# Attention and feed-forward on one core: last tokens in blocks of 256 and 128, zeros written first, one order table replaced by another

## The chip, the cores and the metric

The kernel runs on one core of a Trainium2 chip. A core has five engines with an instruction queue each: PE (the matrix engine, which writes only to PSUM), DVE and ACT (elementwise work), POOL (elementwise work and one kind of DMA) and SP (which here only issues DMAs). They meet through semaphores. Sixteen DMA engines move data between the main memory (HBM) and the on-chip memory (SBUF). The metric is the device time of one execution in microseconds (us), median over the runs of one kernel.

## The reference

Four batches of 1088 tokens, four heads of 32 values each. The attention is linear: a feature map of 64 features per token and head is formed from two projections to 8 values, and so there is no softmax. The result of the attention, 4352 tokens of 128 values, goes through two matrix products with a squared ReLU between them.

```python
def _attn_ref(q, k, v, S1, S2):
    def phi(x):
        a = np.einsum('rd,bhsd->bhsr', S1, x)
        b = np.einsum('rd,bhsd->bhsr', S2, x)
        return np.einsum('bhsi,bhsj->bhsij', a, b).reshape(*x.shape[:-1], r * r)
    q_p, k_p = (phi(q), phi(k))
    kv = np.einsum('bhsf,bhsd->bhfd', k_p, v)
    z = np.sum(k_p, axis=2)
    num = np.einsum('bhsf,bhfd->bhsd', q_p, kv)
    den = np.einsum('bhsf,bhf->bhs', q_p, z)[..., None] + 1e-06
    return num / den

def _moe_ref(x, w_in, w_out):          # x: 4352 x 128, w_in: 128 x 2048, w_out: 2048 x 128
    r = np.maximum(x @ w_in, 0.0)
    return (r * r) @ w_out
```

## The kernel before

**Attention, per batch b (0 to 3).** The steps have names which the order table uses, with the batch as their first number. `ldk`, `ldq`, `ldv` load k, q and v (SP queue, lines 334, 349, 359). `tk` and `tq` transpose k and q on DVE (L380, L442). `ksk` multiplies k by the projections on PE (L390), `kk` transposes the result back (L396) and `kp` forms the 64 features of k on DVE, two instructions of 128x1152 for a batch (L402). `vp` copies v into the layout that the next product needs, a column of ones beside it: two halves for a batch, of three instructions each (L368 and twice L370). `kv` is the product of features and v on PE (L418), `kve` copies it out (L434). For batches 0 and 1 the features of q come from PE: `qr` (L456), a copy `qa` on ACT (L468), a product `qp` on DVE (L473), in three groups of tokens. For batches 2 and 3 they come through the memory: `qr`, `ab` on ACT, `wr` writes a scratch tensor, `rda` and `rdb` read it back spread out (tiles qp and Bq, L512 and L518), `qp` multiplies (L526). `num` is the product with kv (L576), `mx` divides (three DVE instructions, L599 to L601), `tx` transposes on PE (L614) and `xe` copies to xT, the input of the feed-forward, in bf16 (L619).

**Feed-forward, by blocks of tokens.** `SIZES` gives the blocks n = 0, 1, ...: 384, seven of 512, 384. For each block the 16 slices of 128 hidden values are taken W at a time, W = 2 for blocks of more than 256 tokens and W = 4 for smaller ones: `m1.n.m` is W matmuls with w_in into one PSUM tile h of 1024 columns (L642; three such tiles, h0 to h2), `r.n.m` the ReLU from h into an SBUF tile r (ACT, L654, or DVE, L656), `g.n.m` the square (DVE, L669, or ACT, L667), `m2.n.m` W matmuls with w_out that add into the one PSUM tile o (L675). When all are in, `oe` transposes o into an SBUF tile osb on DVE (L682) and four stores `st` (one for each group of 32 partitions, L692) write the block out, more where a block crosses a batch.

**What sets the order.** Nothing is scheduled at run time. The table `PLAN` names every step once, in the order in which it is emitted, with its engine and the buffers it takes; each engine runs its own instructions in that order and waits where a semaphore has not come. A DMA takes one of eight semaphores in turn (DMAHW0 to DMAHW7), whichever of the queues of SP and ACT issues it, and waits until the DMA before it on that semaphore has landed. The last instruction waits for all of them.

**The start.** PE first runs products of a tile of zeros (`heat`, L274), 15 of them around the first work, which need only `zero` (DVE, L212). `ident` (DVE, L228) needs `iota` from POOL. POOL sets constants (`kz`, `z`, `mk`), waits for the first loads with `gate` (L282), issues the loads of the weights w_in (`win`, L285) and w_out (`wout`, L289) on its own DMA queue, and lets the loads of batch 1 and later go with small writes into their targets (`mark0` for k of batch 1, `mark1` for the others, L296).

## Time and profile before

| | before |
|---|---|
| runs: median, lowest, highest | 112.34, 112.20, 112.92 us |
| the profiled execution: its time | 112.42 us |
| its span, first to last instruction | 110.4 us |
| DMA queue of SP and ACT (q1, q10) | 13.95 MB |
| DMA queue of POOL (q0) | 1.05 MB |
| read from and written to HBM | 13.25 MB, 2.79 MB |

The profiled execution lies 0.08 us above the median of the runs, and its span lies 2.0 us below its own time; these 2.0 us are before the first and behind the last instruction. In a row of the timeline stand the start (us from the span's start), the time that the row's instructions took, the engine, the line, the operation, what it writes and reads, and their count; in square brackets how long the engine had been idle before it, and what ended that. "SPq" and "ACTq" are the queues' own work of issuing DMAs. A row of grouped instructions has the busy time, the mean of one in ns, and behind the bar the idle time before them.

### The profile page before, as it was taken

The numbers are of one execution on the slowest core, as the hardware profiler recorded it, in microseconds if no ns is written. First come the engines' busy times: TensorE is split into PE (matmuls) and PEld (weight loads), VectorE is DVE, ScalarE is ACT, GpSimd is POOL, SyncE is SP. The second block draws the span as 40 slices with busy tenths as digits, with TensorE's granted clock in tenths as the row PEclk, the third lists the DMA queues.
The fourth block names the chain that finished last, engine by engine and source line by source line (L and its number), as shares of the span: only waits on it lengthen the run. The fifth ranks groups of instructions, "written<-read, shape, count | busy, mean of one in ns | idle before, by whom it ended". The sixth has DMA issues, their size and how long they took to land.

```text
span 110.4 us, 3529 instructions
## 1 busy us (share of the span) xinstructions
PE 95.6 (87%) x1424; PEld 54.4 (49%) x1436; DVE 94.4 (85%) x157; ACT 86.3 (78%) x111; POOL 19.3 (18%) x59
## 2 busy tenths in 40 slices
PE   0993766999989899999999999998999999999900
PEld 0332754664546557475449354465665444445400
DVE  1439976899999999999999999999899899998720
ACT  5006044899899798899999899999999999999500
POOL 5019990001910280000007200000000000000000
PEclk9999999999999999999999999999999999999995
DMA  2698989994288867576764269720045112041542
GB/s 85 187 232 171 208 181 195 308 270 128 69 212 290 260 195 223 207 215 154 195 159 173 63 167 221 130 39 6 0 85 86 22 29 49 3 71 21 86 82 36
DMA packets 27456, 15.22 MB, mean 138 GB/s; under 512 B 19888, under 2 KB 23344, under 8 KB 27440
## 3 DMA queue, kind: packets, MB, share of 16 engines
q1 hardware_dynamic: 25248, 13.80, 48.2%
q0 software_dynamic: 992, 1.05, 7.0%
q10 hardware_dynamic: 1200, 0.15, 0.8%
q8 instruction: 11, 0.18, 0.7%
q14 instruction: 5, 0.04, 0.1%
HBM read 13.25 MB, written 2.79 MB: 145 GB/s over the span
## 4 chain that ended last, share of the span: by engine, by line
PE 45%; DMA 16%; DVE 13%; POOL 7%; ACT 5%; issue 5%; SPq 3%; POOLq 0%; ACTq 0%
PE o L675 21%; PE h L642 16%; DMA qin<-in_q_dram 6%; ACT r L654 5%; DMA kin<-in_k_dram 4%; DMA qp<-scr 4%; DMA vin<-in_v_dram 3%; PE h L576 3%; DVE kp L402 2%; POOL vp L370 2%; DVE qp L526 2%; DVE g L669 2%; DVE qp L473 2%; DVE osb L682 2%; POOL w_out L289 2%
## 5 line engine op out<-in xcount | busy, mean ns | idle before, releaser
L654 ACT ACTIVATE r<-h 128x1024 bf16<-128x1024 f32 (+1 forms) x64 | 59.2, 976 | 2.5 <-PE h L642 1.6
L642 PE MATMUL h<-xT,w_in 128*128 128x512 bf16 (+1 forms) x136 | 36.3, 367 | 1.7 <-ACT xT L619 0.6
L675 PE MATMUL o<-g,w_out 128*128 128x512 bf16 (+1 forms) x141 | 35.0, 367 | 0.6 <-issue 0.3
L669 DVE TENSOR_TENSOR g<-r 128x1024 bf16<-128x1024 bf16 (+1 forms) x54 | 33.2, 650 | 1.3 <-PE o L675 0.9
L642 PEld LDWEIGHTS <-w_in 128*128 128x128 bf16 x144 | 15.6, 114 | 15.4 <-issue 3.5
L675 PEld LDWEIGHTS <-w_out 128*128 128x128 bf16 x144 | 13.6, 98 | 15.2 <-issue 2.2
L667 ACT ACTIVATE g<-r 128x1024 bf16<-128x1024 bf16 (+1 forms) x18 | 18.3, 1023 | 0.1
L402 DVE TENSOR_TENSOR kp<-kk 128x1152 f32<-128x1152 f32 x8 | 11.7, 1485 | 0.1
L368 POOL COPY vp<-vin 128x512 f32<-128x512 f32 x7 | 5.1, 723 | 35.7 <-DMA Bq<-scr 17.4
L656 DVE TENSOR_SCALAR r<-h 128x1024 bf16<-128x1024 f32 (+1 forms) x8 | 9.5, 1187 | 0.5 <-PE h L642 0.4
L418 PE MATMUL a<-vp,kp 128*32 128x33 f32 (+1 forms) x504 | 7.1, 201 | 1.9 <-DVE kp L402 1.7
L418 PEld LDWEIGHTS a<-vp,kp 128*32 128x32 f32 (+1 forms) x504 | 6.5, 113 | 3.4 <-ACT A L468 2.0
L370 POOL COPY vp<-vtl 32x64 f32<-32x64 f32 x14 | 7.7, 551 | 0.4
L274 PE MATMUL o<-zero 128*128 128x512 bf16 x15 | 5.2, 507 | 2.5 <-DVE zero L212 2.5
L468 ACT COPY A<-h 128x384 f32<-128x384 f32 (+1 forms) x12 | 5.1, 463 | 2.8 <-issue 1.6
L682 DVE STREAM_TRANSPOSE osb<-o 128x512 f32<-128x512 f32 (+1 forms) x9 | 6.1, 681 | 1.3 <-PE o L675 1.3
L456 PE MATMUL h<-qT,SR 32*64 32x192 f32 (+1 forms) x192 | 5.8, 325 | 1.2 <-DVE qT L442 0.9
L473 DVE TENSOR_TENSOR qp<-h,A 128x384 f32<-128x384 f32 (+1 forms) x12 | 6.1, 526 | 0.9 <-ACT A L468 0.9
L380 DVE STREAM_TRANSPOSE kT<-kin 128x1024 f32<-128x1024 f32 (+1 forms) x5 | 5.1, 1017 | 1.9 <-DMA kin<-in_k_dram 1.9
L576 PE MATMUL h<-kvz,qp 128*64 128x66 f32 (+1 forms) x144 | 6.1, 224 | 0.0
L576 PEld LDWEIGHTS h<-kvz,qp 128*64 128x64 f32 (+1 forms) x144 | 5.2, 135 | 1.0 <-issue 0.4
L442 DVE STREAM_TRANSPOSE qT<-qin 128x1088 f32<-128x1088 f32 (+2 forms) x5 | 5.3, 1061 | 0.0
(64 smaller groups left out, 74.2 us busy)
## 6 DMA issues: line engine op xcount, KB each, us to landing
qp<-scr SPq DMA_DIRECT2D x8, 272.0 KB
Bq<-scr SPq DMA_DIRECT2D x16, 136.0 KB
vin<-in_v_dram SPq DMA_DIRECT2D x16, 128.0 KB
qin<-in_q_dram SPq DMA_DIRECT2D x6, 272.0 KB
kin<-in_k_dram SPq DMA_DIRECT2D x4, 288.0 KB
kin<-in_k_dram SPq DMA_DIRECT2D x4, 256.0 KB
out_dram<-osb SPq DMA_DIRECT2D x16, 64.0 KB
scr<-ab SPq DMA_DIRECT2D x8, 68.0 KB
```

The costliest lines, as they stand in the source:

```text
L370: fn(vp[i][32 * c : 32 * c + 32, h, NJ - 1, 0:D], vtl[b][:, h, c])
L402: en.tensor_tensor(out=kp[i][:, pr].rearrange("p j h (x y) -> p (j h) x y", x=R), in0=t[:, :, 1][:, :, None, :].to_broadcast([128, 2 * NJ, ...
L418: nc.tensor.matmul(at(vb)[p : p + m, 33 * pr : 33 * pr + 33], kp[i][:, pr, j, h, m * f : m * f + m], vp[i][:, 2 * pr + h, j, :], start=(j ...
L473: nc.vector.tensor_tensor(out=qp[i][:, pr, t0 : t0 + 2 * n].rearrange("p (m s) -> p m s", m=2), in0=at(hb[pr]).rearrange("p (m s) -> p m s ...
L576: nc.tensor.matmul(t[32 * cc : 32 * cc + 32 * w, 2 * pr : 2 * pr + 2, :], qp[i][:, pr, 32 * c : 32 * c + 32 * w], (kvs if sw else kvz)[b][ ...
L642: nc.tensor.matmul(at(hb)[:, col(w) : col(w) + N], w_in[:, 512 * (ct // E) : 512 * (ct // E) + 512].rearrange("p (c e) -> p e c", e=E)[:, ...
L654: nc.scalar.activation(o, i_, ACTF.Relu)
L656: nc.vector.tensor_scalar_max(o, i_, 0.0)
L667: nc.scalar.activation(at(gb)[:, 0:tot], r, ACTF.Square)
L669: nc.vector.tensor_tensor(out=at(gb)[:, 0:tot], in0=r, in1=r, op=ALU.mult)
L675: nc.tensor.matmul(at(ob)[:, 0:N], w_out[:, ct, :], at(gb)[:, W * N * (mm % SQ_W) + N * w : W * N * (mm % SQ_W) + N * w + N], start=(ct == ...
L682: nc.vector.transpose(at(sbuf)[:, 0:N], at(ob)[:, 0:N])
```

## The change

Five things. `SIZES`: the last block of 384 tokens becomes one of 256 and one of 128; both take W = 4, so that a ReLU or a square of the block of 256 is 1024 columns wide and of the block of 128 is 512. `VP_ENG`: both halves of `vp` of batch 0 stand on ACT, where the second was on POOL. `ident` is kept behind `zero` on DVE. The stores of the last block alternate between the queues of SP and ACT. And `PLAN` is another table: other steps change their engines too (`SKq` goes from DVE to POOL, `xe0.0` from ACT to DVE, the four `kve` of batch 0 swap engines, more of the `xe` stand on ACT), and most steps stand in another place.

```diff
-VP_ENG = "POOL|ACT"
+VP_ENG = "ACT"
-SIZES = [384, 512, 512, 512, 512, 512, 512, 512, 384]
+SIZES = [384, 512, 512, 512, 512, 512, 512, 512, 256, 128]
 PLAN = """
-ldk0.16:SP kz0:POOL z0:POOL iota:POOL ident:DVE zero:DVE heat0:PE:o0 heat1:PE tk0.16:DVE mk:POOL warm:ACT heat2:PE heat3:PE heat4:PE heat5:PE heat6:PE
+zero:DVE heat0:PE:o0 heat1:PE heat2:PE heat3:PE heat4:PE heat5:PE heat6:PE heat7:PE heat8:PE heat9:PE ldk0.16:SP warm:ACT lds0:SP lds1:SP heat10:PE
...
-        ident, iot, 0, op=ALU.is_equal), [o_iota], n=128)
+        ident, iot, 0, op=ALU.is_equal), [o_iota], n=128, after=[o_zero])
...
-                add(f"st{n}.{lo}.{db}", "SP|ACT" if n == len(SIZES) - 1 else "SP", f_st, [o_oe], uses=[sbuf], n=128 * (hi_ - lo))
+                add(f"st{n}.{lo}.{db}", ("SP", "ACT")[db % 2] if n == len(SIZES) - 1 else "SP", f_st, [o_oe], uses=[sbuf], n=128 * (hi_ - lo))
```

Three places of the new order follow, each before and after. The rows give the line, the operation, what it writes and reads (with buffer numbers) and the shape; "x2" is two alike in a row.

First place, the start, on POOL from `gate` on. Before:

```order
L282 COPY gate_147<-vin0_115 64x1
L285 DMA w_in_104<-in_moe_w_in_dram 128x512
L285 DMA w_in_104<-in_moe_w_in_dram 128x1024
L285 DMA w_in_104<-in_moe_w_in_dram 128x512
L296 MEMSET kin1_108 128x2
L368 COPY vp0_127<-vin0_115 128x2x8x32
L370 COPY vp0_127<-vtl0_119 32x2x32 x2
L252 MEMSET vp1_128 128x36
L253 MEMSET vp1_128 64x4x33
L254 MEMSET kT1_124 128x2x32
L289 DMA w_out_105<-in_moe_w_out_dram 128x512
```

And after:

```order
L282 COPY gate_147<-vin0_115 64x1
L285 DMA w_in_104<-in_moe_w_in_dram 128x512 x2
L285 DMA w_in_104<-in_moe_w_in_dram 128x1024
L296 MEMSET kin1_108 128x2
L289 DMA w_out_105<-in_moe_w_out_dram 128x512
L289 DMA w_out_105<-in_moe_w_out_dram 128x2x512
L289 DMA w_out_105<-in_moe_w_out_dram 128x512
L296 MEMSET vin1_116 128x1
L296 MEMSET vtl1_120 32x1
L296 MEMSET qin1_112 128x2
L296 MEMSET kin2_109 128x2
```

The copies of v have left POOL, the three memsets of `z1` stand ahead of `gate` now, and the loads of w_out and the writes of `mark1` follow the loads of w_in at once.

The same place on DVE, which opens with `zero`, as the difference of the two orders:

```order
 L746 UNCONDITIONAL_BRANCH
+L212 MEMSET zero_102 128x256
 L228 TENSOR_SCALAR ident_95<-iot_94 128x128
-L212 MEMSET zero_102 128x256
 L380 STREAM_TRANSPOSE kT0_123<-kin0_107 128x2x256
 L382 STREAM_TRANSPOSE kT0_123<-kin0_107 128x2x32
```

`zero` no longer stands behind `ident`, which needs POOL's `iota`.

Second place, the SP queue around the scratch reads of batch 2 (tiles Bq0 and qp0 from scr0). Before:

```order
L498 DMA scr0_145<-ab0_143 32x2x272
L334 DMA kin2_109<-in_k_dram 128x512
L512 DMA qp0_139<-scr0_145 128x1x544
L518 DMA Bq0_141<-scr0_145 64x1x544
L512 DMA qp0_139<-scr0_145 128x1x544
L518 DMA Bq0_141<-scr0_145 64x1x544
L512 DMA qp0_139<-scr0_145 128x1x544
L334 DMA kin3_110<-in_k_dram 128x512
L518 DMA Bq0_141<-scr0_145 64x1x544 x5
L498 DMA scr1_146<-ab1_144 32x2x272
```

And after:

```order
L518 DMA Bq0_141<-scr0_145 64x1x544 x2
L359 DMA vtl3_122<-in_v_dram 32x4x64
L692 DMA out_0_dram<-osb0_78 32x12x32
L518 DMA Bq0_141<-scr0_145 64x1x544 x2
L512 DMA qp0_139<-scr0_145 128x1x544
L518 DMA Bq0_141<-scr0_145 64x1x544 x2
L692 DMA out_0_dram<-osb0_78 32x12x32
L512 DMA qp0_139<-scr0_145 128x1x544
L518 DMA Bq0_141<-scr0_145 64x1x544 x2
L512 DMA qp0_139<-scr0_145 128x1x544
```

A store of block 0, which waits for `oe0`, stands after the second of the twelve reads now; before, the first store stands behind all twelve.

Third place, the end of the SP queue, with the semaphores that each waits for. Before:

```order
L692 DMA out_0_dram<-osb3_81 32x16x32 [waits DMAHW2_49]
L692 DMA out_0_dram<-osb2_80 32x10x32 [waits DMAHW3_49]
L692 DMA out_0_dram<-osb2_80 32x6x32 [waits DMAHW4_49]
L692 DMA out_0_dram<-osb1_79 32x12x32 [waits DMAHW5_49,DVE_49]
L746 UNCONDITIONAL_BRANCH
```

And after:

```order
L692 DMA out_0_dram<-osb0_78 32x8x32 [waits DMAHW4_49,DVE_49]
L692 DMA out_0_dram<-osb0_78 32x8x32 [waits DMAHW5_49]
L692 DMA out_0_dram<-osb0_78 32x8x32 [waits DMAHW6_49]
L692 DMA out_0_dram<-osb0_78 32x8x32 [waits DMAHW7_49]
L692 DMA out_0_dram<-osb3_81 32x4x32 [waits DMAHW0_49,DVE_49]
L692 DMA out_0_dram<-osb3_81 32x4x32 [waits DMAHW1_49]
L746 UNCONDITIONAL_BRANCH
```

The same place on ACT. Before:

```order
L654 ACTIVATE r3_74<-h1_64 128x768 [waits DVE_49,PE_49]
L654 ACTIVATE r0_68<-h2_65 128x768 [waits DVE_49,PE_49]
L692 DMA out_0_dram<-osb1_79 32x12x32 [waits DMAHW4_49,DVE_49]
L692 DMA out_0_dram<-osb1_79 32x12x32 [waits DMAHW6_49]
L692 DMA out_0_dram<-osb1_79 32x12x32 [waits DMAHW0_49]
L746 UNCONDITIONAL_BRANCH
```

And after:

```order
L654 ACTIVATE r4_76<-h1_64 128x512 [waits DVE_49,PE_49]
L667 ACTIVATE g3_75<-r2_72 128x512 [waits Activation_49]
L654 ACTIVATE r0_68<-h2_65 128x512 [waits DVE_49,PE_49]
L692 DMA out_0_dram<-osb3_81 32x4x32 [waits DMAHW7_49,DVE_49]
L692 DMA out_0_dram<-osb3_81 32x4x32 [waits DMAHW0_49]
L746 UNCONDITIONAL_BRANCH
```

Before, ACT's first store holds DMAHW4, and the next to last SP store waits for it. After, ACT's two stores hold DMAHW7 and DMAHW0, and two of the last three SP stores wait for them, the first of these a store of the block of 256.

## The prediction

> **What bounds the kernel now.** I read the busy times by stretches first, then the timeline of the start and of the end, the chain of waits, and last the groups of instructions for prices. The stretches (us of the span; their length, busy times and counts of PE, PEld, DVE, ACT, POOL; granted clock, DMA share, GB/s):

> ```profile
> 10.00:20.00 10.00, 6.49 (x175) 5.07 (x169) 8.17 (x15) 3.81 (x12) 6.12 (x20) 1.00 0.99 188
> 20.00:40.00 20.00, 18.46 (x405) 11.20 (x409) 19.43 (x34) 18.47 (x28) 5.29 (x10) 1.00 0.74 216
> 80.00:100.00 20.00, 19.86 (x123) 10.36 (x122) 18.97 (x29) 19.61 (x23) 0.00 (x0) 1.00 0.30 50
> 100.00:110.40 10.40, 4.91 (x29) 2.64 (x26) 4.63 (x9) 3.62 (x6) 0.00 (x0) 0.89 0.32 54
> ```

> From 20 on three engines are full together: DVE first (19.43 of 20), PE later (19.86 of 20). The waste lies at the ends: before 20, where PE and ACT stand idle, and behind 105. In between an order can save little, and an engine that gets more work costs about that much. So the sum has three parts: when the feed-forward starts, what is added behind it, and the end.

> **The start.** The timeline's rows up to the first feed-forward product:

> ```profile
> 2.18 0.27 DVE L212 MEMSET zero<- 128x256 uint32 x1
> 2.51 4.79 PE L274 MATMUL o<-zero 128*128 128x512 bf16 x14 [2.51 <-DVE zero L212]
> 5.60 0.71 DVE L380 STREAM_TRANSPOSE kT<-kin 128x512 f32<-128x512 f32 x1 [0.82 <-DMA kin<-in_k_dram]
> 7.22 0.43 PE L390 MATMUL a<-kT,SKk 64*32 64x288 f32 x1
> 8.05 0.48 DVE L396 STREAM_TRANSPOSE kk<-h 128x288 f32<-128x288 f32 x1 [1.74 <-PE h L390]
> 8.46 0.54 DVE L442 STREAM_TRANSPOSE qT<-qin 128x384 f32<-128x384 f32 x1
> 9.25 0.62 ACT L368 COPY vp<-vin 128x512 f32<-128x512 f32 x1 [4.49 <-DMA vin<-in_v_dram]
> 9.39 3.52 DVE L402 TENSOR_TENSOR kp<-kk 128x1152 f32<-128x1152 f32 x2
> 9.78 0.51 ACT L370 COPY vp<-vtl 32x64 f32<-32x64 f32 x2
> 10.28 2.73 POOL L370 COPY vp<-vtl 32x64 f32<-32x64 f32 x2
> 10.31 0.86 ACT L468 COPY A<-h 128x384 f32<-128x384 f32 x2
> 13.40 0.90 DVE L442 STREAM_TRANSPOSE qT<-qin 128x704 f32<-128x704 f32 x1
> 17.00 0.17 DVE L599 TENSOR_SCALAR den<-a 128x12 f32<-128x12 f32 x1
> 17.47 0.56 DVE L601 TENSOR_TENSOR xs<-a,rec 128x384 bf16<-128x384 f32 x1
> 18.90 0.89 DVE L473 TENSOR_TENSOR qp<-h,A 128x320 f32<-128x320 f32 x2 [0.87 <-ACT A L468]
> 19.30 1.14 PE L642 MATMUL h<-xT,w_in 128*128 128x384 bf16 x6 [0.62 <-ACT xT L619]
> ```

> The reader sees PE still busy with products of zeros at 7.30 (2.51 + 4.79), while the transposed k that `ksk0` needs is there at 6.31. And the eight `kp` (shortest, median and longest in ns):

> ```profile
> L402 DVE TENSOR_TENSOR kp<-kk x8: 1318/1356/2215, 9.4 to 70.3; 128x1152 f32<-128x1152 f32 x8
> ```

> *Zeros first.* `zero` no longer waits for `iota`; DVE can write it at about 0.75, where the first engines start, and the products of zeros then end at about 1.05 + 4.8 + one more of up to 0.43 = 6.3, when k is there: 0.87 earlier than now (7.22 against 6.35). The bound below is nothing, if PE runs its zeros slower; above, it cannot pass the arrival of k. I take 0.87. `kk` then starts at about 7.1 and `kp0` at 8.55.

> *The second half of `vp0` on ACT.* This costs ACT 0.62 + 0.51 = 1.13, so its first `qa` moves from 10.31 to about 11.4. DVE meets that only behind `kp0`. On POOL two copies of 32x64 took 2.73 while DVE ran `kp`, and the first `kp` took 2.2 against a median of 1.36; without the copies I price the two `kp` at 2.7 in place of 3.52. Bounds: a gain of 0.8, or nothing, if the issue of weight loads beside them slows DVE as well. I take the gain: the slow rows lie beside copies. [...]

> *The walk.* `kp0` ends at 8.55 + 2.7 = 11.25, not 12.91. `qa` is done at 11.85, so DVE waits 0.6, then does a `qp` (0.89/2 for 320 columns, some 0.55 for 384), the large `tq` (0.90), a second `qp` and two `kve` (0.22 each, a row further down): 14.3. `num0.0` and one `qp` with its copy bring it to 15.3, `mx` (17.00 to 18.03 now, 1.0) to 16.3, `tx` and `xe` to 17.1. The feed-forward starts at about 17.1 in place of 19.30: 2.2 earlier. DVE reaches the same point with `xe0.0` done as well (0.32, which was ACT's) and two `qp` left, as now: 1.85 earlier, from 18.90 to 17.05. The loads of w_out move ahead by nearly 4 us and run beside those of w_in; the DMA issues behind them cost POOL nothing that anybody waits for, and w_in has this time:

> ```profile
> w_in<-in_moe_w_in_dram POOLq DMA_DIRECT2D x2, 128.0 KB, 4.9
> w_in<-in_moe_w_in_dram POOLq DMA_DIRECT2D x1, 256.0 KB, 5.5
> ```

> Issued by 9.7, all of w_in lands by about 15.2, 1.9 before it is needed. That cover is what the earlier w_out could use up.

> **What is added behind the start.** Prices (by shapes, and in the chain of waits: start, time, what):

> ```profile
> L669 DVE TENSOR_TENSOR g<-r 128x1024 bf16<-128x1024 bf16 x41 | 26.6, 683 | 1.2 <-PE o L675 0.9
> L656 DVE TENSOR_SCALAR r<-h 128x1024 bf16<-128x1024 f32 x7 | 8.5, 1220 | 0.1
> L656 DVE TENSOR_SCALAR r<-h 128x768 bf16<-128x768 f32 x1 | 1.0, 957 | 0.4 <-PE h L642 0.4
> L619 DVE COPY xT<-a 128x704 bf16<-128x704 bf16 x1 | 0.5, 519 | 0.0
> ```

> ```profile
> 85.40 0.41 PE a L614 x6
> 96.15 0.86 PE o L675 x4
> 100.02 0.33 PE h L642 x2
> ```

> DVE: its squares grow by 2304 columns, at 26.6/41 = 0.65 for 1024 some 1.5 (1.7 with the smaller shapes' fixed part); one more ReLU of 512 columns, extrapolated from 1.22 and 0.96 to 0.7; from batch 0's second `xe` on two copies of 704 columns fewer, -1.0; two `kve` fewer, -0.45; one more `oe`, 0.2. Sum +1.1. ACT gets less, by the same columns, some 1.3, and is not the bound. PE: a matmul of 384 columns takes 0.165, one of 512 0.215. For 256 I interpolate 0.115; for 128 the transposes, which load new weights each time as well, give 0.41/6 = 0.068. The block of 384 cost 32 x 0.165 = 5.3; now 32 x (0.115 + 0.068) = 5.9: +0.6. Bounds: +0.3 by the slope alone (0.05 for 128), and +1.8 if each of the last 32 waits for its weights at about 0.1. I take 0.6, from the row with the same shape. [...]

> **The end.** The last rows of the timeline, and, of the SP queue's own waits (us in total, times, longest), that of a store for a store:

> ```profile
> 101.24 0.72 DVE L682 STREAM_TRANSPOSE osb<-o 128x512 f32<-128x512 f32 x1 [0.32 <-PE o L675]
> ...
> 104.95 0.58 DVE L682 STREAM_TRANSPOSE osb<-o 128x384 f32<-128x384 f32 x1 [0.57 <-PE o L675]
> 105.56 1.43 ACTq L692 DMA_DIRECT2D out_dram<-osb  x3
> 107.30 0.80 SPq L692 DMA_DIRECT2D out_dram<-osb  x2
> ```

> ```profile
> SPq L692 <- DMA out_dram<-osb: 2.3, 1, 2.3
> ```

> SP stands idle until 107.30, because a store ahead of the last one needs the semaphore of ACT's first store, which lands 1.74 after its issue. The end comes 2.3 after SP's last issue (108.10), 4.9 after the last `oe`. The new table keeps this: ACT's two stores hold DMAHW7 and DMAHW0, and SP has three stores behind them. Issues are shorter (four columns of 32 in place of twelve, 0.3 each against 0.4 to 0.5), so SP issues at 1.5, 1.9 and 2.3 after the last `oe` and the end comes at about 4.75: a gain of 0.15, with -0.3 and +0.5 as bounds. Ahead of it the last steps are smaller: by the two `oe` rows (0.72 for 512, 0.58 for 384) the last falls to some 0.3. But `m2.9` must wait for `oe8` (0.45) to empty the one tile o and then for squares of 0.4 each on DVE, and PE idles some 0.5 there which it did not before. I count these two as +0.2.

> **The sum.** From 105.53, the last `oe`'s end: start -2.0 (PE 2.2, DVE 1.85), added work +0.6 on PE or +1.1 on DVE, of which PE counts late and DVE early, together +0.7; last steps +0.2; stores -0.15; that the other engines' small waits change I cannot sum, and take -0.15 with 1 to both sides. That is -1.4 against the profiled 112.42, so **111.0**. (The profiled execution lies 0.08 above the median.)

> **The rivals.**

> *The lead is lost in the middle.* For it: DVE had 0.6 of idle time in the 20 us from 20 on and gets 1.1 more work; if that hits while DVE is the bound, and PE's small blocks add their 0.6 behind it, then -2.0 + 1.1 + 0.6 + 0.2 - 0.15 leaves -0.3: 112.1. Against it: ACT is freed by 1.3 and DVE has 1.0 of slack in 80 to 100. Late w_in would do the same: beyond 1.9 every us counts in full.

> *The scratch reads of batch 2 come late; slower.* These rows are of the chain (the first is `oe0`), and one of the SP queue's timeline, the first read:

> ```profile
> 32.62 0.49 DVE osb L682
> ...
> 50.93 4.00 DMA qp<-scr
> ...
> 54.96 0.22 DVE kvz L434
> 55.18 1.20 DVE qp L526
> ```

> ```profile
> 34.57 0.58 SPq L512 DMA_DIRECT2D qp<-scr  x1
> ```

> DVE takes up batch 2 the moment the last read has landed, so there is no cover here now. A store that waits for `oe0` stands ahead of ten of these reads; if the reads then end 3 us later, everything behind moves with them: 111.0 + 3 = 114.0. From 1.4 on the kernel is slower than before. Against it: reads run for 12 us from 34.57, and `oe0` ends at about 33 now; it stands some steps later in the new order, but a store held until 36 leaves the reads about where they were.

> *More than the sum.* The start passes on in full, PE's small blocks cost 0.3 and the waits shrink by 1: -2.0 + 0.3 + 0.2 - 0.15 - 1, 109.8.

> *The stores by halves end the wait.* That the change does not do this is in my sum; if ACT's stores landed at once, the end would come 1 earlier, at 110.0. The rows of the queue speak against it.

> **How the numbers follow.** Chances: the forecast 0.55 (110.3 to 111.7), the lost lead 0.20, the late reads 0.15, both better cases together 0.10. About 1%, here 1.1 us, is what a measurement of this kernel can tell from no change, so faster means below 111.2: that holds for 0.7 of the forecast's case and the better ones, 0.39 + 0.10 = 0.49. Slower is the late reads, 0.15; the rest, 0.36, is the same. The range 109.9 to 112.9 leaves out most of the late reads and a small part of the best case.

> **What would show it.** In the new profile: the first products of zeros before 1.3 and the first `ksk` before 6.6; two `kp0` of about 1.36; first feed-forward matmul at 17 to 17.5; the last block's matmuls at 0.07 each; SP's last stores 1.4 to 1.6 after ACT's first. The forecast is wrong if the first feed-forward matmul comes after 18.3, if DVE or PE has a gap of over 1 us between 20 and 100, or if batch 2's `qp` starts later than 55.

## The result, and the profile after

| | before | after |
|---|---|---|
| runs: median, lowest, highest | 112.34, 112.20, 112.92 us | 117.14, 116.14, 117.73 us |
| the profiled execution: its time, its span | 112.42, 110.4 us | 117.73, 115.9 us |

The changed kernel is slower: ratio 1.0413, 95% interval 1.0357 to 1.0470, so 4 to 5 us. The forecast was 111.0. In the text below a ratio is always against the kernel before on the same chip. The ratios leave disturbed runs out and the medians do not, so the two can differ by up to two per cent.

The rows over slices of the span (PE's busy tenths, then the granted clock) and the row of the queue that carries instructions, from the page of after:

```profile
PE   5966763999999099999999999999999999999800
PEclk9999999599999959999999999999999999999985
q8 instruction: 11, 0.18, 0.7%
```

PE, full from 20 on otherwise, has a hole in the fourteenth slice, near 38 us. The granted clock falls to half for one slice twice, near 22 and near 42. Queue 8 has 11 packets of together 0.18 MB, which is 16 KB each. The page of before has the same 11, and the prediction did not ask what they are.

The same by stretches, before and then after (length; busy times and counts of PE, PEld, DVE, ACT, POOL; granted clock, DMA share, GB/s):

```profile
30.00:40.00 10.00, 8.81 (x257) 5.58 (x255) 9.70 (x21) 8.89 (x15) 2.59 (x6) 1.00 0.79 233
40.00:50.00 10.00, 9.84 (x262) 6.24 (x260) 9.86 (x15) 9.24 (x12) 1.07 (x3) 1.00 0.70 216
```

```profile
20.00:30.00 10.00, 10.00 (x123) 5.67 (x122) 8.64 (x15) 8.24 (x12) 1.95 (x5) 0.83 0.57 133
30.00:40.00 10.00, 7.44 (x256) 4.84 (x254) 9.85 (x18) 8.42 (x14) 1.02 (x4) 1.00 0.74 213
40.00:50.00 10.00, 9.30 (x133) 5.67 (x133) 6.38 (x13) 6.03 (x7) 1.68 (x6) 0.83 0.76 192
50.00:100.00 50.00, 49.91 (x654) 27.84 (x653) 49.05 (x74) 48.01 (x56) 4.69 (x6) 1.00 0.41 98
```

From 20 to 30 PE is busy all the time and does only 123 matmuls (155 in before), because they run at half the clock for a third of it (19.93 to 23.34). From 30 to 40 it stands idle for 2.6 us. From 40 to 50 both come together and DVE and ACT run dry behind PE. From 50 on the kernel is as full as it was.

The timeline of after at the first of the two places:

```profile
9.06 2.59 DVE L402 TENSOR_TENSOR kp<-kk 128x1152 f32<-128x1152 f32 x2
15.52 1.01 PE L456 MATMUL h<-qT,SR 32*64 32x192 f32 x31
16.10 0.56 DVE L601 TENSOR_TENSOR xs<-a,rec 128x384 bf16<-128x384 f32 x1
18.66 0.37 PE L456 MATMUL h<-qT,SR 32*64 32x192 f32 x1 [2.12 <-issue]
19.07 0.86 ACT L468 COPY A<-h 128x384 f32<-128x384 f32 x2 [3.67 <-PE h L456]
19.34 0.36 DVE L619 COPY xT<-a 128x384 bf16<-128x384 bf16 x1 [2.28 <-PE a L614]
```

`qr0.1` is 32 matmuls of one kind, with one wait ahead of all. PE does 31, stops for 2.12 us and does the last. No data can be the reason in the middle of such a step, and the profile names none: it writes "issue". ACT waits 3.67 and DVE 2.28 for it; the first feed-forward matmul comes at 19.85.

And at the second place:

```profile
35.58 1.47 PE L418 MATMUL a<-vp,kp 128*32 128x33 f32 x144
36.98 0.97 PE L456 MATMUL h<-qT,SR 32*64 32x160 f32 x32
40.70 0.82 PE L576 MATMUL a<-kvz,qp 128*64 128x66 f32 x10 [2.75 <-DVE qp L473]
```

Here a releaser is named, and wrongly. `num1.0` needs the `kve` copies and `qp1.0`, whose rows end at 38.10 and at 37.57. The `qp` that ends nearest to 40.70 is `qp1.2`, which this step does not read.

Where the time went, from the two profiled executions (differences of the times at which steps begin and end):

| part | before | after | difference | forecast |
|---|---|---|---|---|
| to the first feed-forward matmul | 19.30 | 19.85 | +0.55 | -2.2 |
| from there to the end of `oe6` | 76.51 | 80.28 | +3.77 | +0.15 (0.2 for DVE's smaller lead, 0.1 of added work, -0.15 small waits) |
| from `oe6` to the last `oe` | 9.72 | 10.49 | +0.77 | +0.8 (small blocks 0.6, last steps 0.2) |
| from the last `oe` to the end of the span | 4.91 | 5.26 | +0.35 | -0.15 |

### The profile page after: what moved, and what is told of

Read it like the earlier page. It is cut to its first block, busy times and chain, and to the rows that moved or that the text cites. A ratio compares the mean times of both kernels' runs of the same rounds, so it can differ in the third digit from the quotient of the medians.

```text
span 115.9 us, 3605 instructions
## 1 busy us (share of the span) xinstructions
PE 100.0 (86%) x1468; PEld 58.3 (50%) x1468; DVE 94.7 (82%) x157; ACT 86.1 (74%) x114; POOL 16.4 (14%) x57
## 3 DMA queue, kind: packets, MB, share of 16 engines
q0 software_dynamic: 992, 1.05, 6.0%
## 4 chain that ended last, share of the span: by engine, by line
PE 53%; DMA 16%; DVE 15%; issue 4%; ACT 3%; SPq 3%; POOL 2%; DVEq 0%; POOLq 0%
PE o L675 20%; PE h L642 20%; DMA vin<-in_v_dram 9%; DMA kin<-in_k_dram 6%; PE h L576 4%; DVE g L669 4%; PE a L418 3%; DVE kp L402 2%; DVE qT L442 2%; PE a L576 2%; ACT r L654 2%; DVE osb L682 2%; DMA out_dram<-osb 2%; POOL w_in L285 2%; DVE qp L473 2%
## 5 line engine op out<-in xcount | busy, mean ns | idle before, releaser
L654 ACT ACTIVATE r<-h 128x1024 bf16<-128x1024 f32 (+2 forms) x63 | 58.1, 981 | 7.8 <-PE h L642 7.6
L642 PE MATMUL h<-xT,w_in 128*128 128x512 bf16 (+3 forms) x160 | 38.6, 363 | 1.0 <-DVE xT L619 0.5
L675 PE MATMUL o<-g,w_out 128*128 128x512 bf16 (+3 forms) x160 | 36.0, 350 | 0.3 <-DVE osb L682 0.3
L669 DVE TENSOR_TENSOR g<-r 128x1024 bf16<-128x1024 bf16 (+2 forms) x56 | 34.7, 656 | 1.6 <-ACT r L654 1.5
L642 PEld LDWEIGHTS <-w_in 128*128 128x128 bf16 x160 | 17.3, 116 | 15.5 <-issue 4.1
L675 PEld LDWEIGHTS <-w_out 128*128 128x128 bf16 x160 | 14.8, 98 | 14.0 <-issue 1.2
L667 ACT ACTIVATE g<-r 128x1024 bf16<-128x1024 bf16 (+2 forms) x16 | 16.0, 1007 | 0.1
L656 DVE TENSOR_SCALAR r<-h 128x1024 bf16<-128x1024 f32 (+2 forms) x9 | 10.2, 1128 | 1.5 <-PE h L642 1.3
L402 DVE TENSOR_TENSOR kp<-kk 128x1152 f32<-128x1152 f32 x8 | 10.6, 1345 | 0.0
L368 POOL COPY vp<-vin 128x512 f32<-128x512 f32 x6 | 4.9, 818 | 38.1 <-DMA vin<-in_v_dram 30.7
L468 ACT COPY A<-h 128x384 f32<-128x384 f32 (+1 forms) x12 | 4.9, 465 | 4.2 <-PE h L456 4.1
L380 DVE STREAM_TRANSPOSE kT<-kin 128x1024 f32<-128x1024 f32 (+1 forms) x5 | 5.1, 1025 | 3.3 <-DMA kin<-in_k_dram 3.3
L274 PE MATMUL o<-zero 128*128 128x512 bf16 x16 | 6.3, 565 | 1.2 <-DVE zero L212 1.2
L682 DVE STREAM_TRANSPOSE osb<-o 128x512 f32<-128x512 f32 (+3 forms) x10 | 6.3, 633 | 0.7 <-PE o L675 0.5
L473 DVE TENSOR_TENSOR qp<-h,A 128x384 f32<-128x384 f32 (+1 forms) x12 | 5.9, 522 | 0.8 <-ACT A L468 0.7
L576 PE MATMUL a<-kvz,qp 128*64 128x66 f32 x72 | 3.6, 242 | 3.4 <-DVE qp L473 2.8
L456 PEld LDWEIGHTS h<-qT,SR 32*64 32x64 f32 x192 | 3.8, 131 | 5.3 <-issue 4.2
## 6 DMA issues: line engine op xcount, KB each, us to landing
vin<-in_v_dram SPq DMA_DIRECT2D x16, 128.0 KB
kin<-in_k_dram SPq DMA_DIRECT2D x4, 256.0 KB
```

Source lines behind the costliest of these rows:

```text
L402: en.tensor_tensor(out=kp[i][:, pr].rearrange("p j h (x y) -> p (j h) x y", x=R), in0=t[:, :, 1][:, :, None, :].to_broadcast([128, 2 * NJ, ...
L456: nc.tensor.matmul(at(hb[h // 2])[lo : lo + 64, 512 * half + 256 * x : 512 * half + 256 * x + n], SR[32 * h : 32 * h + 32, x].rearrange("p ...
L473: nc.vector.tensor_tensor(out=qp[i][:, pr, t0 : t0 + 2 * n].rearrange("p (m s) -> p m s", m=2), in0=at(hb[pr]).rearrange("p (m s) -> p m s ...
L576: nc.tensor.matmul(t[32 * cc : 32 * cc + 32 * w, 2 * pr : 2 * pr + 2, :], qp[i][:, pr, 32 * c : 32 * c + 32 * w], (kvs if sw else kvz)[b][ ...
L642: nc.tensor.matmul(at(hb)[:, col(w) : col(w) + N], w_in[:, 512 * (ct // E) : 512 * (ct // E) + 512].rearrange("p (c e) -> p e c", e=E)[:, ...
L654: nc.scalar.activation(o, i_, ACTF.Relu)
```

## The theories and the experiments

The trace has 444 records of matmuls and weight loads on PE before the first stall and 1207 before the second: 763 apart. With PE's other records, its semaphore steps and drains, the counts are 449 and 1217, 768 apart. By the DMA records of after, three packets of queue 8 begin from behind the first stall to the end of the second (at 24.95, 33.02 and 38.31). That is an estimate of 256 records for each packet, and so of 64 bytes of its 16 KB for one. So theory 1: PE's own instructions come by DMA in chunks of 256, and where PE uses a chunk up faster than the next comes, it stops at the border. No run shows when a chunk is asked for; the expectations below reckon from the time at which PE comes into the chunk ahead, which is an assumption of mine. Matmuls of 33 columns, as in `kv`, use up 256 instructions in 1.3 us (144 and their 144 weight loads took 1.47); the feed-forward needs some 20 us for as many (123 matmuls and 122 weight loads from 80 to 100, in a row of the prediction). By the DMA records of after, the chunk for the first border lands at 17.18 and the one for the second at 39.27; PE goes on 1.4 to 1.5 later. The same holds for each of the long stalls shown below (landing, then PE's next matmul): a_heat4 35.42, 36.87; b_heat4 35.14, 36.62; a_heat6 52.75, 54.24. Why the kernel before does not stop at the same count is by this reckoning a matter of pace: there PE took 4.6 us for the 256 records ahead of it (33.34 to 37.91), in after it had done with them in 2.4 (35.99 to 38.35). The fourth packet of queue 8 landed at 36.13 in before, 1.8 ahead of PE's coming to the border, and in after, as said, at 39.27.

The half-rate windows I took for a consequence. The granted clock comes up at 6.28 and falls for 19.93 to 23.34 and 40.41 to 43.82: each 3.41 long, 19.93 is four times 3.41 behind 6.28, and the 17.07 at the full clock between the two are five times 3.41. Each follows the window of 3.41 in which PE stood idle for 2 us and more (2.67 and 2.46).

The rivals: A, the order of PE's steps or late data makes the waits; C, the small blocks carry the loss.

**Later loads (a_late).** In after, the loads of batches 1 and 2 that `mark1` holds back begin at 11.91, before at 16.24. This run holds them back.

```diff
+            if wait is not None:
+                nc.gpsimd.tensor_copy(gate[0:1], wait[0:1, 0:1])
...
-    o_mark["b"] = mark("mark1", ..., o_wout + o_win)
+    o_mark["b"] = mark("mark1", ..., o_wout + o_win, tiles["den0"][1])
```

> The changed kernel, but mark1 (POOL) first copies one value of mx0.0's reciprocal into the gate tile, so the loads of batch 1 and 2 that it holds back are issued near 16, as in the kernel before, instead of 11.9. Theory 1 (PE's own instructions come late: they are fetched over DMA in chunks of 256, and the early loads hold that fetch up): the idle time of PE inside qr0.1 falls from 2.1 to under 0.7, the half-rate window near 20 goes, the second stall near 38 stays; time 117.1 - 2.1 - 1 to 2 of the half-rate window = 113 to 115. Rival A (the order of PE's steps or a late w_in makes the wait): it stays at 2 and the time within 1 of 117.1. Rival C (the small blocks of 256 and 128 carry the loss): within 1 of 117.1 as well.

117.36 us, ratio 1.0428 [1.0367, 1.0490]: no change, where 113 to 115 was expected. In its profile the first stall was only 0.53 and the half-rate window behind it was gone, both as expected; but the stall was 0.22 in the next run (a_kv64), whose loads are early. The first stall varies from run to run, and that early loads cause it is not shown. The second stayed, with its half-rate window (39.81 to 43.23), and the time with it.

**Fewer instructions ahead of the second border (a_kv64).** The `kv` matmuls of batch 1 become 64 columns wide and half as many.

```diff
-KV_M = (64, 32, 32, 32)
+KV_M = (64, 64, 32, 32)
```

> The changed kernel with batch 1's kv matmuls 64 columns wide instead of 32: 72 matmuls and so about 144 PE instructions fewer (kv1 is 72 instead of 144 matmuls) shortly before the second stall, nothing else moved. Theory 1: the chunk border that PE reached at 38.2 lies 144 records later in the program, in m1 and m2 work, where PE needs some 10 records per us: the second stall (2.75 at 37.95) goes or is under 0.7, the half-rate window at 40.4 goes; the first stall stays at 2.1; 113 to 115.5. Rival A (PE waits for qp1 or kve1, its data): the idle time of 2 to 3 us ahead of num1.0 stays, 116.5 to 117.5.

113.38 us, ratio 1.0064 [1.0023, 1.0105]. Of the 4.1% slower, 3.5 are gone, with the small blocks still there: for this part rival C falls. PE at the place, in the timeline of this run:

```profile
33.90 2.29 PE L418 MATMUL a<-vp,kp 128*64 128x33 f32 x72
36.12 0.80 PE L456 MATMUL h<-qT,SR 32*64 32x160 f32 x32
37.37 0.48 PE L576 MATMUL a<-kvz,qp 128*64 128x66 f32 x9 [0.45 <-DVE kvz L434]
```

The wait ahead of `num1.0` fell from 2.75 to 0.45 and is now one for data. The edit itself makes PE slower: 72 wide matmuls take 2.29, the 144 narrow ones took 1.47.

**Both (a_both).** The two edits above together.

> Both edits (late loads, 64-column kv matmuls of batch 1). Theory 1: neither stall, granted clock 1.0 from 6 to 108, the two savings add: 110 to 112.5, no slower than the kernel before's 112.3. Rival A or C: 116 or more.

113.69 us, ratio 1.0072 [1.0027, 1.0116]: as a_kv64 alone, and above the 110 to 112.5 expected. The first stall was still there, 1.08, and no half-rate window followed it. This is the second miss of the idea that holding the loads back helps.

**Another position, the same work (a_heat4).** The strongest test leaves work, order and data alone and only shifts where the borders fall: the warm-up matmuls on the zero tile are cut into four.

```diff
-            nc.tensor.matmul(at(heat_b), zero[:, 0:128], zero, start=True, stop=True)
+            for c in range(0, 512, 128):
+                nc.tensor.matmul(at(heat_b)[:, c : c + 128], zero[:, 0:128], zero[:, c : c + 128], start=True, stop=True)
```

> The changed kernel with each warm-up matmul of 512 columns written as four of 128: the same warm-up time, 90 PE instructions more ahead of the first real matmul, nothing else moved. Theory 1: the chunk borders fall 90 records earlier in the program: the first one inside num0.0 (near 15) instead of the end of qr0.1, with its fetch asked for near 9 instead of 10.4, before mark1's loads are issued, so the first stall shrinks to under 1 or moves to num0.0; the second border falls inside kv1.1, so PE stalls there (line 418) by 2 to 4 us instead of ahead of num1.0; the record count at which PE stops stays 449 and 1217. Rival A (data): both stalls stay where they are, at the end of qr0.1 and ahead of num1.0, at 2 to 2.7 us. Time 113 to 118 by theory 1, 117 by A.

118.59 us, ratio 1.0367 [1.0318, 1.0416]: as slow as after within the intervals. PE in the timeline of a_heat4, at the second place and at the start of the feed-forward:

```profile
17.61 1.71 PE L643 MATMUL h<-xT,w_in 128*128 128x384 bf16 x7 [0.54 <-ACT A L469]
...
32.58 1.53 PE L419 MATMUL a<-vp,kp 128*32 128x33 f32 x129
36.87 0.45 PE L419 MATMUL a<-vp,kp 128*32 128x33 f32 x15 [2.76 <-issue]
```

The stall has moved into the middle of `kv1.1`, where no data is waited for, and the profile now says "issue". The first stall is gone and the feed-forward starts at 17.61 instead of 19.85. Rival A falls here.

**The same shift in the kernel before (b_heat4).** In the kernel before, PE waited 0.29 at the first border and not at the second. If theory 1 holds, the same cut must make one.

> The kernel before, in which no PE stall stands, with each warm-up matmul written as four of 128 columns: 90 PE instructions more ahead of the first real matmul (96 behind heat15), nothing of the work, its order or its data changed. Theory 1 (late instructions): the border at the 1217th instruction now falls at the end of kv1.1, with only 2.7 us of PE work since PE's sequencer went into the chunk ahead of it: a stall of 1.5 to 3 us inside kv1.1 or just behind it near 35, with a half-rate window close behind; 113.5 to 116.5, slower than the kernel before by 1 to 4 per cent. Every rival that explains the loss by the work, its order or its data: 112.3, no stall.

116.24 us, ratio 1.0258 [1.0136, 1.0380]: slower, by warm-up matmuls on zeros that are cut smaller and end no later, and with a feed-forward that starts 0.94 earlier. Behind the stall the clock was at half for two windows, 36.05 to 42.87. PE in the timeline of b_heat4:

```profile
18.36 1.14 PE L643 MATMUL h<-xT,w_in 128*128 128x384 bf16 x6 [0.57 <-ACT xT L620]
...
33.56 0.69 PE L419 MATMUL a<-vp,kp 128*32 128x33 f32 x57
36.62 0.45 PE L419 MATMUL a<-vp,kp 128*32 128x33 f32 x15 [2.37 <-issue]
```

The counts of records (PE's and PEld's x) up to behind the stalls: after at its first and its second, then a_heat4, then b_heat4, each from a stretch that ends inside the stall:

```profile
0.00:18.00 18.00, 12.62 (x222) 7.00 (x222) 10.35 (x22) 5.78 (x15) 7.10 (x38) 1.00 0.83 191
0.00:40.00 40.00, 30.86 (x603) 17.95 (x604) 29.49 (x55) 23.30 (x42) 10.07 (x45) 0.96 0.76 188
```

```profile
0.00:36.00 36.00, 28.33 (x604) 20.06 (x604) 27.25 (x49) 21.06 (x37) 11.30 (x45) 1.00 0.84 206
```

```profile
0.00:36.00 36.00, 27.19 (x604) 18.94 (x604) 27.43 (x49) 21.30 (x36) 13.51 (x47) 1.00 0.82 208
```

1207, 1208 and 1208 records: ahead of `num1.0` in one, inside `kv1.1` in the other two, and these two in different orders. What PE was doing differs; how many instructions it had done does not.

**A shift meant to help (a_heat6).** As a_heat4, with six pieces of 96 columns.

```diff
-            for c in range(0, 512, 128):
+            for c in range(0, 512, 96):
```

> The changed kernel with each warm-up matmul written in six pieces of 96 columns (the last of 32): 150 PE instructions more ahead of the first real matmul, 160 behind heat15; the kv matmuls of batch 1 stay 32 wide, nothing else moves. Theory 1 (late instructions; a border stalls where PE has used up the 256 instructions before it faster than the next chunk comes, about 4.5 us): the border of the second stall now falls in the middle of the dense stretch kv1.0, kv1.1, qr1.2, num1.0, so that the chunk before it and the one behind it each hold some 70 instructions of slow m1 and m2 work; no idle time of PE over 0.7 us between 10 and 45 but the waits for data that stand in every run; first FFN matmul at 17.4 to 17.8; time 110.5 to 112. Theory 1b (it is the number of kv instructions alone, and only fewer of them help): second stall stays at 2 to 3, 114 to 116. Rival A (data): as after, 116 to 118.

113.73 us, ratio 1.0106 [1.0043, 1.0169], above the 110.5 to 112 expected. At both old places PE's waits are under 0.7, but its profiled execution (115.0) has a new stall of 2.99 at 51, behind `kv2`:

```profile
50.08 0.83 PE L420 MATMUL a<-vp,kp 128*32 128x33 f32 x72
50.84 0.41 PE L644 MATMUL h<-xT,w_in 128*128 128x512 bf16 x1
54.24 0.62 PE L644 MATMUL h<-xT,w_in 128*128 128x512 bf16 x2 [2.99 <-issue]
```

It lies 758 records behind 1208, again about three chunks on. The mechanism held, and the shift was badly chosen: only the borders up to 45 us were considered. The two runs below, with the same shift, stop at the same count, 1966, for 1.07 and 1.88.

**The split undone (a_heat6_384).** As a_heat6, with the last 384 tokens as one block, its eight steps standing where the four and four stood.

```diff
-SIZES = [384, 512, 512, 512, 512, 512, 512, 512, 256, 128]
+SIZES = [384, 512, 512, 512, 512, 512, 512, 512, 384]
```

> As a_heat6, with the last 384 tokens in one block again, its eight steps in the places of the four and four of the two small blocks. What the split costs: by the sum of the prediction (+1.7 in work, of which 0.6 on PE, -0.9 in the last steps) within 0.3 of a_heat6 either way; if the small blocks carry a part of the loss, 0.5 to 1.5 us faster than a_heat6; if the split pays, slower by 0.3 to 1. The end behind the last oe should stay at 5.2 to 5.3 with SP's stores behind ACT's.

111.91 us, ratio 0.9968 [0.9930, 1.0006], 1.4% below a_heat6. Behind the last `oe` its span lasts 3.81 in place of 5.26, and nothing of that was expected. SP's and ACT's last stores, in the timeline of a_heat6_384:

```profile
107.38 0.83 SPq L692 DMA_DIRECT2D out_dram<-osb  x2
107.38 0.91 ACTq L692 DMA_DIRECT2D out_dram<-osb  x2
```

Both queues issue at once. By the profiles, the one block makes the stretch from `oe6` to the last `oe` 0.38 longer (10.87 against 10.49) and the end 1.45 shorter. In after, SP's last two come behind a wait of 2.0, as in this row of the SP queue's waits there (us in total, times, longest):

```profile
SPq L692 <- DMA out_dram<-osb: 2.0, 1, 2.0
```

A store of the block of 256 stands ahead of them and has the semaphore of ACT's first store, eight DMAs back. Without the four stores of that block none of SP's last stores has the semaphore of one of ACT's.

**The order of the last four stores (a_heat6_st).** As a_heat6, with the order of before: SP one, ACT three.

> As a_heat6, with the last four stores in the order of the kernel before (SP one, ACT three) instead of ACT, SP, ACT, SP. If SP's late stores (0.35 of the tail) come from the order of the four, the end behind the last oe falls from 5.26 to 4.9 and the time by 0.3; if they come from the stores of the block of 256 just ahead of them on SP, it stays at 5.2 or more.

114.21 us, ratio 1.0191 [1.0108, 1.0274]. The end behind the last `oe` stayed at 5.26, so it is the stores ahead that matter; the time alone would not have told, since it also holds what the stall at 51 does.

**The stores by halves in the kernel before (b_halves).** Two stores of block 6 go to POOL's queue so that the ring of eight is not in the way.

```diff
-st6.2944.2:SP st6.3264.2:SP ... st8.3968.0:SP st8.3968.1:ACT st8.3968.3:ACT st8.3968.2:ACT
+st6.2944.2:POOL st6.3264.2:POOL ... st8.3968.3:ACT st8.3968.2:SP st8.3968.1:ACT st8.3968.0:SP
```

> The kernel before with the last four stores by halves, ACT, SP, ACT, SP, and two earlier stores of block 6 issued by POOL instead of SP, so that none of SP's last stores shares a semaphore with one of ACT's. If SP's last stores are held by the landing of ACT's first (2.3 us of wait in the kernel before), the end behind the last oe falls from 4.9 to 3.8 and the time by 1.1 to 111.1 to 111.4; if they are held by the stores ahead of them in SP's queue, it falls by at most 0.5.

110.62 us, ratio 0.9875 [0.9825, 0.9925]: 1.4 us faster, the fastest kernel of this study, and a little more than the 111.1 to 111.4 expected. The end behind the last `oe` is 3.48 in place of 4.91 (expected 3.8). Of SP's waits, the one of a store for a store is gone and this one is left:

```profile
SPq L692 <- DVE osb L682: 3.8, 2, 2.7
```

**The second half of vp0 on ACT, alone (b_vp).** The kernel before with that one step of the change.

```diff
-VP_ENG = "POOL|ACT"
+VP_ENG = "ACT"
-vp0.0:ACT
+vp0.0:ACT vp0.1:ACT
```

> The kernel before with vp0.1 on ACT behind vp0.0 instead of on POOL, nothing else. POOL comes to its later memsets, to mark1 and so to batch 1's loads some 4 us earlier, and the kv matmuls of batch 0 no longer wait for POOL. Theory 1: more traffic ahead of the first fetch, and PE at its border (the 449th instruction) earlier: idle 1 to 2.5 us there instead of 0.6, a half-rate window possible behind it; 112.5 to 114.5. Rival A (only data counts): first FFN matmul 0.5 to 1 earlier than 19.3 and 111.5 to 112.2.

112.49 us, ratio 0.9997 [0.9953, 1.0042]: neither. The two `kp0` take 2.63 in place of 3.52 and the feed-forward starts at 18.98, 0.32 earlier; PE's wait at the border is 0.55 (0.29 in before). The end does not move by an amount that can be measured.

**Sum of the repairs (a_kv64_384, a_h8_kv64_384).** After with 64-wide `kv1` and the last block whole; then the same with the warm-up matmuls cut into eight, a shift chosen over all borders.

> The changed kernel with both losses found so far taken out: batch 1's kv matmuls 64 wide (no second stall) and the last 384 tokens in one block. If the losses add: 113.1 (a_kv64 against the kernel before) less 1.5 (the split, from a_heat6 and a_heat6_384) = 111.0 to 111.8, the forecast of the prediction, and 0.5 to 1.3 faster than the kernel before. If the split's cost belongs to the a_heat6 pair's stalls alone: 112.8 to 113.4.

> As a_kv64_384, with each warm-up matmul in eight pieces of 64 columns: 210 PE instructions more ahead of the first real matmul (224 behind heat15), a shift at which no border of the trace of a_kv64 has under 7.5 us of PE work since its fetch could be asked for. Theory 1: no stall at all, the first one inside qr0.1 (0.7 to 2.4) gone too: first FFN matmul at 17.5 to 18.2 instead of 19, and 110.0 to 111.2. Against: warm-up matmuls of 64 columns end sooner and leave PE idle ahead of the first real matmul, so that the clock comes up later or drops: then 111 to 112.5.

112.93 us, ratio 0.9951 [0.9904, 0.9998], and 111.49 us, ratio 0.9933 [0.9899, 0.9968]. In the second no wait of PE between 10 and 100 is over 0.7, the granted clock is 1.0 from 6.46 to 108.86, and its feed-forward starts at 18.30. Its median is 0.9 below the kernel before. Both medians lie above what was expected if the losses add (111.0 to 111.8, then 110.0 to 111.2). In the profile of the first, a stall of 1.22 inside `qr0.1` was left, with the clock at half from 19.23 to 22.65. The two repaired kernels cannot be told apart, and both stay behind b_halves.

## Why the prediction was wrong, step by step

- **Zeros first: half right.** The zero products started at 1.19, as forecast. They were to end in time for `ksk0` at 6.35; it came at 7.03. "4.8 + one more" took the time of 14 zero products that ran partly at the full clock. In after the clock rose at 6.28, in before at 5.76, though the zeros started 1.3 earlier: the rise did not follow the start. The 15 took 5.91 in place of 5.2. The early start also has a price that the prediction does not count. PE then stood idle for 1.2 to 2.0 ahead of `qr0.0`, against 0.8 to 0.9 in the four profiles with zeros behind `ident`, and in three of the ten with zeros first (a_kv64, a_heat6_384, a_heat6_st) the clock fell to half near 11. In a_kv64 `kv0` took 3.63 there, in after 2.51.
- **vp0.1 on ACT: right.** The two `kp0` took 2.59 (forecast 2.7). That it is worth 0.9 at this place (less where the copies stayed on POOL and `kp0` took 3.04 and 3.17, in b_heat4 and b_halves) and nothing at the end (b_vp) was not foreseen.
- **The walk: right up to 16.5, and there it failed.** `kp0` ended at 11.65 (11.25) and `mx`'s last instruction at 16.66 (16.3). Then PE stopped for 2.12 inside `qr0.1`. The forecast's 17.1 for the first feed-forward matmul took it that PE waits only for data. Where no border falls there, after starts it at 17.61 (a_heat4).
- **The gain of the start was mis-sized as well.** Without the border, after's start of 17.61 (a_heat4) is 1.69 ahead of before's 19.30, and 0.75 ahead of 18.36, where the border is out of the way on both sides (b_heat4); neither is 2.2. Of the 0.94 between before and b_heat4 the border was only some 0.3: `mx` had already ended 0.64 later in before (18.03 against 17.39), behind slower `kp0` (3.52 against 3.04), and why is open. In a_kv64, the second stall gone, the start gained 0.29. The row that would have told of the border stood in the timeline of before, the last two matmuls of a step of 32, small:

```profile
17.97 0.43 PE L456 MATMUL h<-qT,SR 32*64 32x160 f32 x2 [0.29 <-issue]
```

- **"That the other engines' small waits change I cannot sum, and take -0.15 with 1 to both sides": the step that failed.** What was left out there is a wait of PE for its own instructions, 2.75 at the second border, with the clock at half for 3.41 behind each of after's two stalls. Taking the second stall away with a_kv64 changed the ratio from 1.0413 to 1.0064, 3.9 us, though that edit costs PE 0.8. The range's upper end of 112.9 had no room for it.
- **Added work in the middle: too high.** From the first feed-forward matmul to the end of `oe6`, a_kv64 took 76.10, before 76.51. DVE's extra 1.1 does not show there.
- **The small blocks and the last steps: right in the sum, by luck.** +0.77 against 0.6 + 0.2. The rows of after, last block and the one ahead of it:

```profile
106.23 1.03 PE L675 MATMUL o<-g,w_out 128*128 128x256 bf16 x8
...
108.91 1.36 PE L675 MATMUL o<-g,w_out 128*128 128x128 bf16 x16 [0.32 <-DVE osb L682]
110.30 0.32 DVE L682 STREAM_TRANSPOSE osb<-o 128x128 f32<-128x128 f32 x1 [0.47 <-PE o L675]
```

  A row's time holds the whole of its last matmul, so its mean is too high as a price. From start to start, where PE does not wait, matmuls of 256 columns came 0.109 apart and of 128 columns 0.056 (priced at 0.115 and 0.068), those of 384 in before 0.163. So the two blocks cost 32 x (0.109 + 0.056) = 5.3 and the one block 5.2: almost nothing, not +0.6. What made the 0.77 instead: PE's waits in this stretch grew by 0.5 (0.49 ahead of `m2.9` and 0.30 inside it, in after), its matmuls by 0.5, since another share of them stands behind `oe6` in the new order, and the last `oe` is 0.26 shorter. The prediction had the waits at 0.5.
- **The stores: -0.15 forecast, +0.35 measured**, inside the bounds of -0.3 and +0.5. SP had three stores left behind the wait, as the prediction said. They were issued from 1.54 to 2.85 behind the last `oe`, 0.3 to 0.4 each with up to 0.2 between them, where 1.5 to some 2.4 was forecast; the end followed 2.4 later, as before (2.3).
- **The rivals.** Late reads did not decide: batch 2's `qp` ran at 57.7 in after, behind the sign of 55 that the prediction set, but DVE was busy with other work up to it, and it ran at 52.9 in a_kv64 with the same order of reads and stores. In no profile is there a wait of PE for w_in. "The stores by halves end the wait" was worth 1.4 where they were freed of the ring (b_halves). The rival that came true was not on the list.

Open: how long a chunk takes to come. By the records of after, its transfer took 0.9 to 1.5, but it began 4.8 (first border) and 2.3 (second) after PE's count of records reached the chunk ahead; in before the second began 1.9 after. That a chunk is asked for at that point was assumed and is not shown, and that DMA traffic makes it late was only argued: a_late, made to show it, did not. Nor did I separate what the half-rate windows cost from the stalls ahead of them.

## What to carry to other kernels

On a PE stream with short matmuls in a row, count instructions: here 256 in 2.4 us ran into a stall and 256 in 4.6 us did not, and stalls showed as idle time "by issue" in the middle of a step (2.12 in after, 2.76 in a_heat4, 2.37 in b_heat4), at a count that stayed at 1207 or 1208 when the program around it moved. An order, or a faster start, can be right in every wait for data and still lose by where the borders fall (b_heat4, ratio 1.0258). Fewer and wider matmuls in the dense stretch (a_kv64, from 1.0413 to 1.0064), or a shift by dummy matmuls ahead of it (a_h8_kv64_384, no wait over 0.7 between 10 and 100), were the repairs here, and a shift must be judged over all later borders (a_heat6, 2.99 at 51). When two queues share a ring of semaphores, look at what the last stores have to wait for (a wait of 2.0 in after; b_halves, without one, 1.4 us faster than before) before moving them between queues.
